# Reordering VectorE's work at the start of a fused layer: the third x tile's statistics placed behind the PSUM copy of the second tile's transposed x

## The chip, the cores and the metric

The kernel runs on one core of one Trainium2 chip. The metric is device time in microseconds (us) of one execution; lower is better. "Span" is the time from the first to the last instruction in the trace; the device time is about 1.8 us longer than the span. Each timed execution also reports its mean granted TensorE clock. 3.41 us at half clock in a span of 366 us lower the mean by 0.5 x 3.41 / 366 = 0.0047, so such an execution reads 0.995, as the profiled one of the kernel before does, instead of 1.00.

Engines: PE is TensorE's matmuls, PEld its weight loads, DVE is VectorE, ACT is ScalarE, POOL is GpSimd, SP is SyncE, which issues most DMAs.

## The reference, cut to what matters

```python
x = A_x                                     # 1 x 2048 x 576, bf16
h = x + attention(layernorm(x), wqkv, wo)   # 32 heads, each token sees 8 tokens, 2 apart
h2 = h + mlp(layernorm(layernorm(h)), w1, b1, w2, b2)   # 576 -> 4608 -> 576, gelu
return h2
```

The 2048 tokens are 16 tiles of 128. The change touches only the first 10 us: layernorm of the first x tiles, their transposition, and the first k and v products.

## The kernel before

Tiles are named by position in `EVEN`, the list of even tiles: "first tile" is `EVEN[0]`. An even tile is centered on VectorE, transposed on TensorE into PSUM, copied to SBUF (`xnT`), and multiplied with wqkv. The factor 1/sigma is applied when ScalarE evacuates the product from PSUM.

```python
# loads are issued in this order on SyncE's queue (t = 1 is k, t = 2 is v, t = 0 is q)
load_x(EVEN[0:1]); load_x(EVEN[1:2])
# ... the two tail pieces of wk go through ScalarE's queue
load_wqkv(1, 0, 2); load_wqkv(1, 2, KF)      # wk
load_x(EVEN[2:3]); load_x(EVEN[3:4])         # third and fourth x tile
load_wqkv(2, 0, 2); load_wqkv(2, 2, KF)      # wv
for r in range(2):
    load_wqkv_half(nc.sync, 2, r)
load_x(EVEN[4:6])                            # fifth and sixth x tile
# ... further loads; then 13 matmuls of constants that keep TensorE busy from 0.78 us

def ln1_even_stats(gi):      # bn_stats x2, bn_aggr on VectorE
    ...
def ln1_even_center(gi):     # x - mean, on VectorE
    ...
def ln1_even(gi):
    ln1_even_stats(gi)
    ln1_even_center(gi)

def ln1_even_rstd(*gis):
    for gi in gis:
        ...
        nc.vector.tensor_scalar(out=veps[:], ...)              # var + eps, VectorE
        rstd_of[EVEN[gi]] = ln_rstd(veps, f"ln1_{gi}", 1)[:, 0:1]   # pow(-0.5), GpSimd

def tr_x(js, tag):
    ...                      # transposes on TensorE into a PSUM pair
    copy = nc.vector.tensor_copy if j == EVEN[1] else nc.scalar.copy
    copy(out=xnT[j][:, k0:k1], in_=...)      # the second tile's copy is VectorE's
```

A "visit" makes the products of two (tile, k/v/q) pairs, each in two halves. The second half must come after the whole first half, and a no-operation on GpSimd carries that order: it waits for the first half's last matmul, and TensorE's second half waits for it.

```python
def marker(mm_ins):
    nop = nc.gpsimd.nop().ins
    tc.add_manual_dep(nop, mm_ins.name, sync_dep, ...)
    return nop

def visit(makes, ...):
    def first(make):
        duos.append(make())
        marks.append(marker(phase(duos[-1], 0, None)))
    ...                                      # first halves of all, then:
    phase(duos[n], 1, marks[n])              # second half, behind the marker
    duos[n]["evac"]()                        # ScalarE: PSUM -> SBUF, times 1/sigma
```

The instructions of each engine run in the order in which the program states them: in the trace of before, VectorE's copy, whose input was ready at 6.38 us, ran at 8.11 us, behind the statistics stated ahead of it. The start of the main part reads:

```python
ln1_even(0)                  # first tile: statistics and centering on VectorE
ln1_even_act(1)              # second tile: statistics on ScalarE, centering on VectorE
seq = [(j, t) for t in (1, 2) for j in EVEN[:2]] + [(j, 1) for j in EVEN[2:]] + ...

ln1_even_stats(2)            # third tile
tr_x(EVEN[0:1], "D")
tr_x(EVEN[1:2], "C")
ln1_even_center(2)
ln1_even_rstd(0, 1)
for qd in range(len(seq) // 2):
    duos = [qkv_duo(*seq[2 * qd]), qkv_duo(*seq[2 * qd + 1])]
    visit(duos, hooks.get(qd), ...)
    call(after.get(qd, ()))  # from here: other tiles' statistics, attention of finished tiles
```

Later parts: attention's first product of a tile on VectorE; SyncE's queue, which reloads the k of that tile and then stores, transposes and loads the odd tiles' x (`xd`, `xnT`); and the output projection `pw`, whose input `oT` is written by VectorE, stored to DRAM and loaded back transposed.

## Time and profile before

| | before |
|---|---|
| median of 3 timed runs | 366.63 us (366.52 to 367.52) |
| profiled execution | 367.94 us, span 366.2 us, mean clock 0.995 |
| TensorE busy | 360.4 us, 98% of the span |
| VectorE busy | 299.1 us, 82% |
| ScalarE busy | 229.1 us, 63% |

The profile's chain follows the work that ended last back from the end, with each engine's share of the span. The first line is for engines:

```profile
PE 88%; DVE 7%; DMA 3%; SPq 1%; issue 0%; POOL 0%
```

TensorE is the bound, and any idle TensorE time before the end is a candidate. The view of waits for TensorE lists only these (who waited, for whom: us in total, times, longest):

```profile
PE pq L215 <- DVE xnT L270: 1.3, 1, 1.3
PE busy L772 <- PEq L1061: 0.8, 1, 0.8
PE pw L215 <- DMA oT<-td: 0.2, 1, 0.2
```

The first is the target of the change. The timeline of VectorE around it (start, duration, engine, line, operation; in brackets the idle time before the instruction and what ended it):

```profile
4.57 0.36 DVE L789 TENSOR_SCALAR q_all<-x_all,ln_nmean 128x576 bf16<-128x576 bf16 x1
7.13 0.82 DVE L149 BATCH_NORM_STATS2 ln_stats<-x_all 128x6 f32<-128x288 bf16 x2 [2.20 <-DMA x_all<-in_A_x_dram]
7.98 0.21 DVE L150 BATCH_NORM_AGGREGATE ln_mv<-ln_stats 128x2 f32<-128x12 f32 x1
8.11 0.44 DVE L270 COPY xnT<-xt_pt 128x640 bf16<-128x640 bf16 x1
8.46 0.36 DVE L789 TENSOR_SCALAR q_all<-x_all,ln_mv 128x576 bf16<-128x576 bf16 x1
8.74 0.15 DVE L819 TENSOR_SCALAR ln_veps<-ln_mv 128x1 f32<-128x1 f32 x1
8.80 0.14 DVE L819 TENSOR_SCALAR ln_veps<-ln_sq 128x1 f32<-128x1 f32 x1
```

VectorE idles 2.20 us, because the third tile's statistics (L149) are next and its load has not landed. The copy (L270) stands behind them, although TensorE's timeline shows that its transposes (L182, L186) ended at 6.14 + 0.24 = 6.38 us:

```profile
6.14 0.24 PE L186 MATMUL xt_pt<-ident,q_all 128*64 128x128 bf16 x1
6.31 0.83 PE L215 MATMUL pq<-wq_sb,xnT 64*128 64x288 bf16 x8
6.97 0.30 PE L215 MATMUL pq<-wqh_sb,xnT 64*128 64x288 bf16 x2
8.60 0.95 PE L215 MATMUL pq<-wq_sb,xnT 64*128 64x288 bf16 x8 [1.33 <-DVE xnT L270]
9.34 0.45 PE L215 MATMUL pq<-wqh_sb,xnT 64*128 64x288 bf16 x2
9.58 2.95 PE L215 MATMUL pq<-wq_sb,xnT 64*128 64x288 bf16 x24
```

Note the last line too: 24 matmuls in 2.95 us. The windows view of three equal stretches says why; they are cut where the trace's own clock records begin (5.43, 8.85 and 12.26 us). Its columns are the stretch and its length, then busy time and instruction count of PE, PEld, DVE, ACT and POOL, then the granted clock, the DMA share and GB/s:

```profile
5.43:8.85 3.42, 2.09 (x24) 1.14 (x24) 1.69 (x7) 0.75 (x2) 0.00 (x0) 1.00 1.02 315
8.85:12.26 3.41, 3.41 (x34) 2.21 (x30) 2.48 (x10) 1.19 (x2) 1.08 (x2) 0.50 1.00 321
12.26:15.67 3.41, 3.41 (x50) 2.27 (x48) 3.27 (x14) 2.13 (x4) 1.06 (x2) 1.00 1.07 359
```

After a stretch with TensorE busy 2.09 of 3.42 us, the clock was halved for exactly one stretch of 3.41 us. Three more lines are VectorE's first product of attention, its first sum with the projection, and TensorE's wait for oT:

```profile
26.86 2.56 DVE L343 TENSOR_TENSOR prod<-kv_ring,q_all 128x4608 bf16<-128x4608 bf16 x1 [0.22 <-ACT q_all L310]
54.83 0.76 DVE L459 TENSOR_TENSOR h<-pw,x_all 128x576 f32<-128x576 f32 x1 [0.52 <-PE pw L215]
88.14 0.54 PE L215 MATMUL pw<-wo_sb,oT 64*128 64x288 bf16 x6 [0.21 <-DMA oT<-td]
```

### The profile page before, as it was taken

What the parts mean: (1) busy time and instruction counts of PE and PEld (TensorE: products, weight loads), DVE (VectorE), ACT (ScalarE), POOL (GpSimd) and SP (SyncE); (2) the same over time, 40 slices, a digit from 0 to 9 for tenths busy, and PEclk for the clock granted to TensorE, in tenths of its full rate; (3) what the DMA queues carried; (4) which work ended last, traced back from release to release, by engine and by line L of the source; (5) the groups of instructions that cost most, each with busy time, mean ns of one, the idle gap of its engine ahead of it and who ended that gap; (6) DMA issues with size and microseconds to landing.
All of it is one profiled execution on the core that took longest, in us unless ns stands there. A gap on an engine that the chain in (4) does not pass through costs nothing.

```text
span 366.2 us, 11427 instructions
## 1 busy us (share of the span) xinstructions
PE 360.4 (98%) x4899; PEld 291.3 (80%) x4899; DVE 299.1 (82%) x422; ACT 229.1 (63%) x507; POOL 38.3 (10%) x47
## 2 busy tenths in 40 slices
PE   7999999999999999999999999999999999999996
PEld 3677877788778877887788778878887888778874
DVE  4889999999899999999999898989995599710331
ACT  4579865799545674468546864686468646625630
POOL 1232003000120030102110021011101010100000
PEclk9899999999999999999999999999999999999999
DMA  7977989973444853630452145303631452030001
GB/s 241 306 197 260 236 216 215 370 270 71 137 107 80 165 198 70 108 98 34 129 109 71 38 103 117 90 32 92 130 72 35 81 93 56 3 90 18 2 2 33
DMA packets 61908, 43.70 MB, mean 119 GB/s; under 512 B 31889, under 2 KB 60177, under 8 KB 61857
## 3 DMA queue, kind: packets, MB, share of 16 engines
q1 hardware_dynamic: 59968, 41.13, 41.2%
q0 software_dynamic: 1728, 1.77, 4.7%
q8 instruction: 38, 0.62, 0.7%
q10 hardware_dynamic: 160, 0.07, 0.1%
q14 instruction: 14, 0.11, 0.1%
HBM read 21.10 MB, written 12.42 MB: 92 GB/s over the span
## 4 chain that ended last, share of the span: by engine, by line
PE 88%; DVE 7%; DMA 3%; SPq 1%; issue 0%; POOL 0%
PE pm L215 34%; PE po L659 27%; PE pq L215 11%; PE po L574 10%; PE pw L215 5%; DVE prod L349 1%; DVE prod L343 1%; DMA oT<-td 1%; DMA x_all<-in_A_x_dram 1%; DVE prod L395 1%; DVE ln_stats L149 1%; DVE prod L401 1%; PE xt_pt L182 1%; SPq L104 0%; DMA td<-q_all 0%; DVE h L459 0%
## 5 line engine op out<-in xcount | busy, mean ns | idle before, releaser
L555 ACT ACTIVATE h_all<-pm,b_sb 128x256 f16<-128x256 f32 (+1 forms) x288 | 108.3, 496 | 77.1 <-PE pm L215 77.1
L215 PE MATMUL pm<-hnT,w_sb 64*128 64x256 bf16 x2304 | 143.0, 269 | 0.0
L215 PEld LDWEIGHTS <-w_sb 64*128 64x128 bf16 x2304 | 111.7, 94 | 15.1 <-issue 1.7
L659 PEld LDWEIGHTS <-h_all 128*128 128x128 f16 x544 | 52.3, 98 | 15.3 <-issue 2.5
L215 PE MATMUL pq<-wq_sb,xnT 64*128 64x288 bf16 x768 | 56.0, 288 | 1.3 <-DVE xnT L270 1.3
L215 PEld LDWEIGHTS <-xnT 64*128 64x128 bf16 x864 | 42.3, 96 | 13.4 <-DVE xnT L270 1.6
L349 DVE TENSOR_TENSOR prod<-prod 128x2304 bf16<-128x2304 bf16 (+1 forms) x64 | 44.2, 691 | 2.1
L659 PE MATMUL po<-w2a_sb,h_all 128*128 128x288 bf16 (+1 forms) x312 | 43.6, 286 | 0.0
L395 DVE TENSOR_TENSOR prod<-kv_ring,probs 128x4608 bf16<-128x4608 bf16 x16 | 40.9, 2553 | 1.3 <-DMA kv_ring<-kv_dram 0.9
L343 DVE TENSOR_TENSOR prod<-kv_ring,q_all 128x4608 bf16<-128x4608 bf16 x16 | 40.8, 2549 | 0.4 <-ACT q_all L310 0.2
L215 PE MATMUL pm<-hnT,w1h_sb 64*128 64x256 bf16 x288 | 39.2, 269 | 0.0
L401 DVE TENSOR_TENSOR prod<-prod 128x2304 bf16<-128x2304 bf16 (+1 forms) x32 | 33.8, 1057 | 1.0
L574 PEld LDWEIGHTS <-h_all 128*128 128x128 bf16 x288 | 27.9, 98 | 7.9 <-issue 1.0
L479 POOL TENSOR_TENSOR ln_rstd<-ln_var,mhalf 128x1 f32<-128x1 f32 x13 | 14.2, 1091 | 178.0 <-ACT ln_var L478 178.0
L574 PE MATMUL po<-w2a_sb,h_all 128*128 128x288 bf16 x224 | 28.5, 286 | 0.0
L659 PEld LDWEIGHTS <-kv_ring 128*128 128x128 f16 x240 | 23.5, 98 | 5.9
L659 PE MATMUL po<-w2b_sb,h_all 128*128 128x288 bf16 (+1 forms) x152 | 22.2, 286 | 0.0
L639 DVE TENSOR_TENSOR kv_ring<-h_all 128x1536 f16<-128x1536 f16 (+3 forms) x10 | 6.9, 686 | 16.0 <-ACT h_all L555 16.0
L215 PE MATMUL pw<-wo_sb,oT 64*128 64x288 bf16 x256 | 19.5, 283 | 0.2 <-DMA oT<-td 0.2
L162 POOL TENSOR_TENSOR ln_rstd<-ln_veps,mhalf 128x1 f32<-128x1 f32 (+2 forms) x14 | 12.5, 903 | 51.2 <-DVE ln_veps L156 30.6
L215 PEld LDWEIGHTS <-oT 64*128 64x128 bf16 x288 | 13.4, 94 | 5.3 <-issue 1.7
L459 DVE TENSOR_TENSOR h<-pw,x_all 128x576 f32<-128x576 f32 x16 | 11.5, 752 | 6.5 <-PE pw L215 6.5
(107 smaller groups left out, 374.6 us busy)
## 6 DMA issues: line engine op xcount, KB each, us to landing
w_sb<-in_B_w_dram SPq DMA_DIRECT2D x6, 768.0 KB, 5.7
kv_ring<-kv_dram SPq DMA_DIRECT2D x28, 144.0 KB, 2.8
w2a_sb<-in_B_w_dram SPq DMA_DIRECT2D x4, 1008.0 KB, 6.7
kv_dram<-kv_ring SPq DMA_DIRECT2D x13, 288.0 KB, 3.6
out_dram<-o_sb SPq DMA_DIRECT2D x15, 144.0 KB, 2.2
td<-q_all SPq DMA_DIRECT2D x14, 144.0 KB, 2.2
td<-hn SPq DMA_DIRECT2D x14, 144.0 KB, 1.8
x_all<-in_A_x_dram SPq DMA_DIRECT2D x12, 144.0 KB, 2.8
```

The lines of the kernel that those rows point to most:

```text
L162: nc.gpsimd.tensor_tensor(out=rstd[:], in0=veps[:], in1=mhalf[:].to_broadcast([P, n]), op=ALU.pow)
L215: last = nc.tensor.matmul(duo["g"][r ^ swap][i], lhsT=lhsT, rhs=rhs, start=(swap == 0 and i == 0 and kt == 0), stop=(swap == 1 and kt == K ...
L343: nc.vector.tensor_tensor(out=prod[:], in0=k_ring[j % 2], in1=q_all[:, j, :].unsqueeze(1) .to_broadcast([P, W, D]), op=ALU.mult)
L349: nc.vector.tensor_tensor(out=prod[:, :, o * H:o * H + n], in0=prod[:, :, a * H:a * H + n], in1=prod[:, :, c * H:c * H + n], op=ALU.add)
L395: nc.vector.tensor_tensor(out=prod[:].rearrange("p w (d h) -> p w d h", h=H), in0=v_ring[j % 2].rearrange("p w (d h) -> p w d h", h=H), in ...
L401: nc.vector.tensor_tensor(out=prod[:, 0:n, :], in0=prod[:, 0:n, :], in1=prod[:, n:2 * n, :], op=ALU.add)
L459: nc.vector.tensor_tensor(out=h[:].rearrange("p (g c) -> p g c", g=2), in0=pw[:, :, 0:HALF], in1=x_of(j).rearrange("p (g c) -> p g c", g=2 ...
L479: nc.gpsimd.tensor_tensor(out=rstd[:], in0=var[:], in1=mhalf[:], op=ALU.pow)
L555: pace[0] = nc.scalar.activation(out=hT(grp)[:, f, 0:N], in_=ps[:, r, i * N:(i + 1) * N], func=ACT.Gelu_apprx_tanh, bias=b1_sb[:, f:f + 1] ...
L574: nc.tensor.matmul(banks[half], lhsT=hT(grp)[:, f, i * P:(i + 1) * P], rhs=w2_rows(f)[:, half * HALF:(half + 1) * HALF], start=(f == 0), s ...
L639: nc.vector.tensor_tensor(out=s_slot(t, m0, m1), in0=a, in1=b, op=alu)
L659: nc.tensor.matmul(bank, lhsT=l, rhs=r, start=start, stop=stop, skip_group_check=True)
```

## The change

The intent is to let the copy, and the small var + eps operations of the first two tiles, run while VectorE waits for the third tile's load anyway.

```diff
-        ln1_even_stats(2)
+        ln1_even_rstd(0, 1)
         tr_x(EVEN[0:1], "D")
         tr_x(EVEN[1:2], "C")
-        ln1_even_center(2)
-        ln1_even_rstd(0, 1)
+        ln1_even(2)
         for qd in range(len(seq) // 2):
```

No instruction is added or removed. On VectorE three instructions move ahead of the statistics; GpSimd's order does not change.

## The prediction

> **What bounds the kernel now.** The engine table gives TensorE (PE) 360.4 of 366.2 us busy (98%), VectorE (DVE) 299.1. The chain of waits is 88% PE, 7% DVE, 3% DMA. PE has two idle stretches of note: 1.33 us from 7.27, released by DVE's copy of the second tile's transposed x, and 0.21 at 88, released by a DMA. Its clock was halved once: the windows view shows 0.50 from 8.85 to 12.26 us, where 24 matmuls took 2.95 us that later take 1.64. [...]
>
> **Why the gap.** The timeline shows DVE idle from 4.93 to 7.13 us: the third tile's statistics wait for that tile's load (landed 7.10). The queue is in order; the copy stands behind them and runs at 8.11 (0.44 us), although its transposes ended near 6.4.
>
> **What the change does.** Same 391 DVE rows; only the order at the start changes: two small var+eps operations (0.15 us each) and the copy (0.44 us) go into DVE's idle hole before the load lands. The copy should run at 6.4 to 6.9. The statistics stay bound by their load, near 7.13.
>
> **What that is worth.**
> - PE: the gap goes (1.3 us), and probably the half-clock window (36 matmuls in 4.05 us, about 2.35 at later rates: 1.7 us). The next visit then meets the loads of the v weights, which landed at 8.43 to 9.75 (new waits 0.2 to 0.5 us). PE should be 2.5 to 2.8 us early by the transposes that now start at 12.58.
> - Most of it is lost again. From 11.11 us (load of the fifth tile) DVE is a nearly unbroken stream to 88; up to 64 only three of its pauses can shrink: 0.52 (26.47), 0.22 (26.86), 0.52 (54.83) = 1.26 us. PE's next meeting with it is the projection at 88.14, which waits for oT, stored and read back after DVE's sum at 81.4. So PE waits there 1 to 1.6 us more. From there PE has no slack: at most about 1.3 us of the span is left.
> - [...] An untouched clock alone would win that 1.26 us, leaving the change almost nothing. The times (366.52, 366.63, 367.52), beside 367.94 for the profiled, throttled execution, allow that the median was unthrottled. I mix: 1.3 us if throttled, 0.1 if not.
>
> **Predicted: 366.0 us, range 364.9 to 366.9 (8 in 10).** Faster by over 2%: 0.01; within 2%: 0.98; slower by over 2%: 0.01.
>
> **What will show it.** Right: the copy at 6.4 to 6.9 us, PE without a gap over 0.5 us before 12, granted clock 1.00 between 8 and 13, transposes of the third tile near 10 us, DVE's first product of attention near 26.1 instead of 26.86, the wait for oT near 88 grown to over 1 us, span about 365. Wrong: a half-clock stretch within the first 15 us; a DVE stream that starts no earlier; the projection at 88.14 moving by the full 2.7 us.
>
> **What would make it wrong.** The longer wait near 87 us may itself [...] halve the clock (1.7 us lost: no gain, or 0.5 us slower). Shifted ScalarE evacuations could move paced loads. Or all timed runs are throttled, and the gain is the full 1.3 us.

The gap (1.3 us) and the half-clock stretch (1.7 us), less the new waits (0.2 to 0.5 us), are the 2.5 to 2.8 us; the cap leaves about 1.3 us, for a throttled execution, and 0.1 us stands for one at full clock. Mixed, they take about 0.6 us off the 366.63 us of before: 366.0 us.

## The result, and the profile after

| | before | after |
|---|---|---|
| median of 4 runs of the same rounds | 366.57 us (365.90 to 367.52) | 365.19 us (365.08 to 365.28) |
| ratio | | 0.996, interval 0.9938 to 0.9983 |
| profiled execution | span 366.2 us, clock 0.995 | span 363.3 us, clock 1.00 |

A ratio is the mean time of one kernel's fast runs over that of the other's in the same rounds, so it is not quite the ratio of the medians. The interval excludes 1, so the change is faster, by about 0.4% (in microseconds the interval is 0.6 to 2.3).

The two profiles differ by 2.9 us of span, twice as much as the medians. That is the first warning: the profile of before fell in an execution with a half-clock stretch, and most executions have none (e1 below).

The chain after is TensorE nearly alone:

```profile
PE 98%; DMA 1%; DVE 0%; ACT 0%; SPq 0%; issue 0%
```

TensorE's waits shrink to the one at the program's start:

```profile
PE busy L772 <- PEq L1060: 0.8, 1, 0.8
```

VectorE's timeline after: the small operations and the copy run in the hole, and the copy now waits for the transposes themselves:

```profile
4.76 0.15 DVE L819 TENSOR_SCALAR ln_veps<-ln_mv 128x1 f32<-128x1 f32 x1
5.35 0.15 DVE L819 TENSOR_SCALAR ln_veps<-ln_sq 128x1 f32<-128x1 f32 x1 [0.45 <-ACT q_all L811]
6.83 0.49 DVE L270 COPY xnT<-xt_pt 128x640 bf16<-128x640 bf16 x1 [1.33 <-PE xt_pt L186]
7.24 0.81 DVE L149 BATCH_NORM_STATS2 ln_stats<-x_all 128x6 f32<-128x288 bf16 x2
```

TensorE's timeline after has no gap, and 24 matmuls take 1.71 us; the transposes of the third tile start at 9.98 us, against 12.58 before:

```profile
6.73 0.67 PE L215 MATMUL pq<-wq_sb,xnT 64*128 64x288 bf16 x8
7.23 0.29 PE L215 MATMUL pq<-wqh_sb,xnT 64*128 64x288 bf16 x2
7.38 0.66 PE L215 MATMUL pq<-wq_sb,xnT 64*128 64x288 bf16 x8
8.01 1.71 PE L215 MATMUL pq<-wq_sb,xnT 64*128 64x288 bf16 x24
9.98 0.28 PE L182 MATMUL xt_pt<-ident,q_all 128*128 128x128 bf16 x2
```

The windows view of the same two stretches of time: busy throughout, no half clock from 6.59 us on.

```profile
5.43:8.85 3.42, 3.42 (x44) 2.29 (x44) 2.02 (x7) 0.84 (x3) 0.67 (x2) 1.00 1.02 321
8.85:12.26 3.41, 3.41 (x46) 2.14 (x42) 2.86 (x11) 2.32 (x4) 0.16 (x1) 1.00 1.07 347
```

The 1.00 of its first line must be read with care. This trace's first clock record begins at 6.59 us, and the column says 1.00 before it by default. The first transposes show that TensorE was still slow there (after, then before, whose record begins at 5.43 us):

```profile
5.90 0.71 PE L182 MATMUL xt_pt<-ident,q_all 128*128 128x128 bf16 x5
5.75 0.45 PE L182 MATMUL xt_pt<-ident,q_all 128*128 128x128 bf16 x5
```

That is why the copy ran at 6.83 us here, and at 6.08 us in e2, where the two tiles' groups of five transposes took 0.44 and 0.45 us instead of the 0.69 and 0.71 here.

And the three later places:

```profile
25.09 2.55 DVE L343 TENSOR_TENSOR prod<-kv_ring,q_all 128x4608 bf16<-128x4608 bf16 x1
52.47 0.75 DVE L459 TENSOR_TENSOR h<-pw,x_all 128x576 f32<-128x576 f32 x1
85.27 0.66 PE L215 MATMUL pw<-wo_sb,oT 64*128 64x288 bf16 x8
```

So TensorE is 12.58 - 9.98 = 2.60 us early at the third tile, and still 88.14 - 85.27 = 2.87 us early at the projection. VectorE is 1.77 us early at attention and 2.36 us early at 52 us. In this pair of traces the lead was not lost on VectorE, as the prediction had said it would be.

### The profile page after: what moved, and what is told of

Its sections match the earlier page's. It is cut to its first block, busy times and chain, and to the rows that moved or that the text cites. A ratio compares the mean times of both kernels' runs of the same rounds, so it can differ in the third digit from the quotient of the medians.

```text
span 363.3 us, 11427 instructions
## 1 busy us (share of the span) xinstructions
PE 359.0 (99%) x4899; PEld 292.3 (80%) x4899; DVE 299.1 (82%) x422; ACT 229.3 (63%) x507; POOL 39.4 (11%) x47
## 3 DMA queue, kind: packets, MB, share of 16 engines
q0 software_dynamic: 1728, 1.77, 4.6%
## 4 chain that ended last, share of the span: by engine, by line
PE 98%; DMA 1%; DVE 0%; ACT 0%; SPq 0%; issue 0%
PE pm L215 39%; PE po L659 27%; PE pq L215 15%; PE po L574 10%; PE pw L215 5%; PE xt_pt L182 1%; DMA x_all<-in_A_x_dram 1%; PE xt_pt L186 0%; ACT q_all L810 0%; PE h_pt L182 0%; PE o_pt L182 0%; DVE o_sb L690 0%; SPq L104 0%; DVE q_all L789 0%; PE h_pt L186 0%; PE o_pt L186 0%
## 5 line engine op out<-in xcount | busy, mean ns | idle before, releaser
L215 PE MATMUL pq<-wq_sb,xnT 64*128 64x288 bf16 x768 | 54.4, 283 | 0.0
L162 POOL TENSOR_TENSOR ln_rstd<-ln_veps,mhalf 128x1 f32<-128x1 f32 (+2 forms) x14 | 13.4, 962 | 47.9 <-DVE ln_veps L156 31.6
L503 POOL DMA_DIRECT2D x_all<-h x12 | 10.9, 1060 | 54.6 <-DMA x_all<-in_A_x_dram 25.0
```

Source lines behind the costliest of these rows:

```text
L162: nc.gpsimd.tensor_tensor(out=rstd[:], in0=veps[:], in1=mhalf[:].to_broadcast([P, n]), op=ALU.pow)
L215: last = nc.tensor.matmul(duo["g"][r ^ swap][i], lhsT=lhsT, rhs=rhs, start=(swap == 0 and i == 0 and kt == 0), stop=(swap == 1 and kt == K ...
L503: ins = nc.gpsimd.dma_start(out=x_of(j), in_=h_of.pop(j)[:], accum_op=ALU.add).ins
```

## The experiments

All experiments have five rounds. The kernel before was timed in every set, on the same chip, and the ratios below are against it. Because sets fell on different chips, I compare kernels of different sets by their distance from the kernel before of their own set. I take before's executions at a clock above 0.996 for this. Their medians in the four sets are 365.89, 366.06, 365.80 and 365.93 us.

### e1: the kernel before, as a subject of its own

No edit; one profile and five timed runs with their clocks.

> The kernel before, unchanged, run as a subject of its own, so that every timed run shows its granted clock. Theory A (the gap of 1.33 us in TensorE's matmuls also costs a half-clock window in some executions): runs fall in two groups, clock 0.995 or 0.996 with a span near 366, and clock 1.00 with a span near 364.3 to 365. Rival B (the clock is a bystander): the spans do not follow the clock; spread of about 1.5 us within equal clocks. The ratio to the kernel before is 1.000 within 0.002 either way.

Measured: 366.14, 366.06, 365.95 and 365.46 us at clock 1.00, and 367.31 us at 0.995; ratio 0.9996. The profiled execution took 2120.91 us; it is left out. Its trace has a span of 2119.1 us, the 13 matmuls that open the kernel take 12.13 us instead of the 4.11 in before, and TensorE is busy for 20.00 of 20 us in three samples, from 500, 1000 and 2000 us; the clock column reads 1.00, and why it was slow is not shown. In the four sets together the kernel before ran 42 times. Seven executions read 0.995, with a median of 367.73 us (367.27 to 368.08). The other 35 have a median of 365.93 us, and all but one lie between 365.46 and 366.48. The two groups do not overlap but for that one, 367.30 us at 0.999, which the clock does not explain. Theory A's two groups are there; the clock costs 367.73 - 365.93 = 1.8 us, in one execution of six.

### e2: only the statistics move

```diff
-        ln1_even_stats(2)
         tr_x(EVEN[0:1], "D")
         tr_x(EVEN[1:2], "C")
-        ln1_even_center(2)
+        ln1_even(2)
         ln1_even_rstd(0, 1)
```

> Only the statistics move behind the copy; the two var+eps operations stay where they were, behind the third tile's centering. Theory A (the early copy is all of the gain): as fast as the changed kernel, near 365.2 us, 1.2 to 1.6 us under the kernel before, no gap of TensorE over 0.5 us before 12 us. Rival C (the gain comes from the early 1/sigma of the first two tiles, which frees PSUM evacuations on ScalarE): no gain or less than 0.5 us.

Measured: 365.54 us (365.30 to 365.76), ratio 0.9978 (0.9956 to 1.0), no execution at 0.995; 0.35 us under before's clock-1.00 median. By the ratio the gain is 0.8 us, between the two theories' numbers; by the medians it is about 0.4 us, within rival C's. The trace has something that neither had named. The waits of TensorE in this kernel:

```profile
PE pq L215 <- POOLq L225: 1.0, 1, 1.0
PE pq L215 <- DMA wq_sb<-in_A_wqkv_dram: 0.4, 1, 0.4
```

TensorE now waits for GpSimd's queue at L225, the marker. The 1/sigma operations of the first two tiles stand ahead of the markers in that queue; their inputs come at 8.69 + 0.14 us, behind the third tile's centering, and TensorE's second halves start at 8.95 us. The copy alone moves the wait from VectorE's queue to GpSimd's.

### e3: only the var + eps operations move

```diff
+        ln1_even_rstd(0, 1)
         ln1_even_stats(2)
         tr_x(EVEN[0:1], "D")
         tr_x(EVEN[1:2], "C")
         ln1_even_center(2)
-        ln1_even_rstd(0, 1)
```

> Only the two var+eps operations move to the front; the statistics stay ahead of the copy. Theory A: the time of the kernel before within 0.4 us, and the gap of 1.3 us in TensorE stays. Rival C: most of the 1.4 us gain.

Measured: 366.30 us (365.75 to 367.65), ratio 1.0008 (0.9983 to 1.0032); two of six executions at 0.995. TensorE's gap is still 1.3 us in the view of waits. No gain: this half of the change does nothing alone, and rival C falls.

### e4: the kernel before, with the gap filled

```diff
+        def fill():
+            more = psum_pair("D", "busy_more")
+            for _ in range(5):
+                nc.tensor.matmul(more[:, 0, :], lhsT=ones[:, 0:P], rhs=ones[:], start=True, stop=True)
+
+        hooks[0] = {1: fill}
         for qd in range(len(seq) // 2):
```

> The kernel before with five unused matmuls of 512 columns in the gap [...], so that the gap stays in time but TensorE does not idle in it. Results stay right. Theory A: the clock stays at 1.00 from about 6 us on in every run, and the time is that of the best runs of the kernel before, 0.5 to 1.2 us under its median, with a spread of 0.3 us; the changed kernel stays a little better. Rival B (only the 1.33 us of gap counts, not the clock): no change from the kernel before.

Measured: 365.84 us (365.45 to 365.91), ratio 0.9985 (0.9966 to 1.0005); all six clocks at 0.999 or 1.00. No execution is in the slow group (with one in six expected, none of six is no proof), and the median equals before's clock-1.00 executions (365.89 in this set). In its trace the five unused matmuls took 1.26 us. The expected 0.5 to 1.2 us under before's median did not come, because that median is itself an execution at full clock.

### e7 and e12: the gap doubled, then the doubled gap filled

e7 puts two unused statistics operations ahead of the copy in the kernel before; e12 adds nine unused matmuls in the gap, as in e4.

```diff
         ln1_even_stats(2)
+        junk(2)          # two bn_stats on the first tile's x, result unused
         tr_x(EVEN[0:1], "D")
```

> The kernel before with two more unused statistics operations (0.82 us) ahead of the copy, so that TensorE's gap grows from 1.33 to about 2.15 us. Theory A: executions with a half-clock window become the majority, and their share, not only 0.8 us of delay, moves the time: median 1.5 to 2.5 us over the kernel before, fast-clock executions 0.5 to 0.8 us over its own. Rival B: 0.5 to 0.8 us slower in all executions, with no more of them at 0.995.

> The kernel with the doubled gap (2.07 us in its trace, 5 of 6 executions at clock 0.994 or 0.995, median 368.27 us) with nine unused matmuls of 512 columns in the gap [...]. The gap in useful work stays as long; only TensorE's idleness goes. Theory A [...]: no execution at 0.995, and 366.5 to 367.2 us, 1.1 to 1.8 us under the kernel with the doubled gap. Rival B (only the length of the gap counts): 368 us or more.

Measured: e7 took 368.27 us (367.08 to 368.63), ratio 1.0048 (1.0026 to 1.007). Five of its six executions read 0.994 or 0.995 (368.01 to 368.63 us); the sixth, at 1.00, took 367.08. e12 took 366.54 us (366.51 to 366.83), all five at 0.998 or above; in its trace the nine unused matmuls took 2.14 us. The windows view of e7, two stretches of 3.41 us:

```profile
6.98:10.39 3.41, 1.34 (x21) 0.85 (x21) 3.03 (x11) 0.00 (x0) 0.50 (x1) 1.00 0.95 283
10.39:13.80 3.41, 3.41 (x31) 1.99 (x25) 3.20 (x13) 1.48 (x2) 0.58 (x2) 0.50 1.00 325
```

and of e12, the same two:

```profile
6.98:10.39 3.41, 3.41 (x33) 1.79 (x31) 3.34 (x12) 0.00 (x0) 0.84 (x2) 1.00 1.01 313
10.39:13.80 3.41, 3.41 (x50) 2.26 (x47) 3.23 (x13) 2.44 (x4) 1.01 (x3) 1.00 1.07 358
```

The useful work is held up about as long in both: the second tile's matmuls start at 9.52 us in e7 and at 9.18 us in e12. Above before's full-clock executions of their own sets the two stand at 2.21 and 0.61 us, so 1.6 us go with TensorE's idleness (at most 0.3 of it with the later start). This is the clearest evidence that the clock is a cause, and that TensorE's idleness in the gap triggers it. The share of half-clock executions rises with the gap: none of the ten of the changed kernel, 7 of 42 at 1.33 us, 5 of 6 at 2.07 us.

### e5: the changed kernel again

> The changed kernel once more, to stand beside the others of this set. Expected 365.1 to 365.3 us, no execution with the clock at 0.995, spread under 0.4 us.

Measured: 365.36 us (365.06 to 366.27), ratio 0.9976 (0.9955 to 0.9997), none at 0.995, 0.70 us under before's 366.06. One execution at 366.27 (clock 0.999) makes the spread wider than expected.

### e6 and e9: VectorE made longer in the changed kernel

Two or six unused statistics operations (0.82 or 2.45 us) ahead of attention's first product:

```diff
-            5: [..., c_(ln1_bias, 9), c_(att_qk_a, A[0])],
+            5: [..., c_(ln1_bias, 9), c_(junk, 2), c_(att_qk_a, A[0])],     # 6 in e9
```

> The changed kernel with two unused statistics operations (0.82 us together) on VectorE just ahead of attention's first product. In its trace oT landed at 85.16 us and TensorE took it at 85.27, so VectorE's stream has about 0.1 us of slack there. Theory D (VectorE's stream is at its limit in the changed kernel): slower by 0.5 to 0.8 us, near 365.9, with a wait of TensorE for oT near 86 us. Rival P (only TensorE bounds it): slower by less than 0.2 us.

> The changed kernel with six unused statistics operations (2.45 us) on VectorE ahead of attention's first product. With two of them (0.82 us) the median rose by only 0.26 us, because the transposing load of oT, issued later, took 3.1 us instead of 4.0. Theory S (VectorE's stream has about 1 us of slack in the changed kernel, then it binds): 1.0 to 1.9 us slower than the changed kernel, near 366.4 to 367.2 us, with a wait of TensorE for oT of 0.8 to 1.6 us near 86 us. Theory D (no slack): 2.3 us or more. Rival P (VectorE does not bind at all): under 0.4 us.

Measured: e6 365.62 us (365.14 to 367.61), ratio 0.9988, 0.26 us over the changed kernel in the same set, which is not clear of the spread of either; e9 366.73 us (366.29 to 369.33), ratio 1.0033. e9's four executions at clock 1.00 have a median of 366.38 us, 0.58 over before's 365.80, while the changed kernel was 0.70 under its own: a cost of about 1.3 us for 2.45 us of work. So theory S holds in size: VectorE has some slack, up to roughly a microsecond, and then it binds. The place is not the one I expected. e9's wait of TensorE for oT does not appear; what appears in its timeline is a wait for the odd tiles' transposed x, twice, 1.0 us in all; the longer wait is the 0.69 us before this line:

```profile
37.97 0.66 PE L215 MATMUL pq<-wq_sb,xnT 64*128 64x288 bf16 x8 [0.69 <-DMA xnT<-xd]
```

Two of e9's six executions read 0.995 and took 369.04 and 369.33 us; neither was profiled, so where their clock fell is not known.

### e8: the markers ahead of 1/sigma

As e2, with the same order on VectorE, but 1/sigma behind the markers in GpSimd's queue.

```diff
         ln1_even(2)
-        ln1_even_rstd(0, 1)
+        hooks[0] = {2: c_(ln1_even_rstd, 0, 1)}   # after the first visit's two markers
```

> As the kernel that moved only the statistics, with the same order on VectorE, but the first two tiles' 1/sigma stand behind the two marker operations in GpSimd's queue instead of ahead of them. In that kernel TensorE waited 0.98 us for GpSimd's queue. Theory E (the early var+eps operations of the change matter only because the markers stand behind 1/sigma in GpSimd's queue): the wait is gone, the transposes of the third tile come near 10 us, and the time is that of the changed kernel within 0.2 us. Rival C (the later 1/sigma costs by itself, through ScalarE's PSUM evacuations): it stays at 365.5 us, with a new wait of TensorE for ScalarE near 10.5 us.

Measured: the wait for GpSimd's queue is gone from TensorE's waits, which in this kernel are:

```profile
PE busy L772 <- PEq L1060: 0.8, 1, 0.8
PE pq L215 <- DMA wq_sb<-in_A_wqkv_dram: 0.5, 1, 0.5
```

That settles what e2's wait was. The time does not settle its worth: 365.65 us, but from 364.92 to 366.25, ratio 0.9982 (0.9958 to 1.0005), 0.41 us under before where the changed kernel of the same set was 0.70 under. In e8 ScalarE's first evacuation waits for 1/sigma until 9.44 us, against 8.77 in the changed kernel, but TensorE did not wait for ScalarE. Theory E is shown for the wait and open for the time. The third tile's transposes came at 10.52 us and not near 10, and the traces say why: in after, e5, e6, e8, e9 and e11 they start 0.25 to 0.26 us after the last piece of the v weights has landed (9.73 and 9.98 us in after, 10.10 and 10.35 in e5, 10.26 and 10.52 in e8). Once the copy and the markers are early, this landing ends last, and in e8's profiled execution it was late.

### e10: the v weights' landing taken out (wrong result)

```diff
-                c0 = t * D + g * HALF
-                return xt[sl, kt, :], (wq_sb[sl, kt, c0:c0 + HALF] if kt < KF else wqh_sb[sl, t, :])
+                w = 1 if (j, t) == (EVEN[0], 2) else t
+                c0 = w * D + g * HALF
+                return xt[sl, kt, :], (wq_sb[sl, kt, c0:c0 + HALF] if kt < KF else wqh_sb[sl, w, :])
```

> Wrong result on purpose: in the changed kernel the first tile's v is multiplied with the k weights, which are there, so that TensorE's third visit no longer meets the v weights' loads (waits of 0.2 to 0.5 us in the traces so far). Theory V (the landing of the v weights took the rest of the closed gap): 0.2 to 0.5 us faster than the changed kernel, near 364.9 us, transposes of the third tile near 9.6 us. Rival D (VectorE or oT holds the end of the stage): no gain, and a longer wait for oT near 86 us.

Measured (result wrong): 364.65 us, ratio 0.9961 (0.9937 to 0.9985), 1.15 us under before's 365.80, against 0.70 for the changed kernel in its set: about 0.45 us came from no longer meeting the v weights (a difference of two sets). In its trace the third tile's transposes start at 9.16 us, before the last piece of these weights lands (9.81). But 365.63 and 367.19 us stand beside five runs between 364.40 and 364.74. The 367.19 one was profiled, at clock 1.00, and its timeline shows what it met:

```profile
39.09 0.66 PE L215 MATMUL pq<-wq_sb,xnT 64*128 64x288 bf16 x8 [2.75 <-DMA xnT<-xd]
```

TensorE was there at 36.34 us, only 0.75 us earlier than in the changed kernel's trace, where the load of xnT landed at 37.05 us and TensorE took it at 37.09. In this execution the load landed at 39.05 us, 2.0 us later. VectorE was not the reason: it began attention at 25.11 us, against 25.09. SyncE's queue was 1.3 us behind at the reload of k before it (29.33 against 28.05), and the load itself took 5.5 us instead of 4.3; why is not known. So the odd tiles' x is a second limit right behind the first, with 0.04 us to spare in the changed kernel's trace. It may also explain the rare long executions of other kernels at full clock, but those were not profiled.

This trace also corrects the picture of the clock. TensorE idles 2.75 us, longer than the 2.07 us in e7, and no half-clock stretch follows. Two stretches of 3.41 us that meet inside the gap:

```profile
34.50:37.91 3.41, 1.85 (x32) 1.25 (x26) 3.24 (x6) 2.89 (x5) 0.00 (x0) 1.00 1.11 275
37.91:41.32 3.41, 2.23 (x38) 1.95 (x40) 3.18 (x8) 0.46 (x2) 0.00 (x0) 1.00 0.77 230
```

TensorE was busy 1.85 of 3.41 us in the first, less than the 2.09 of 3.42 us after which before's clock was halved. So busy time alone does not decide.

### e11: the v weights loaded ahead of the fourth tile

```diff
         load_x(EVEN[2:3])
-        load_x(EVEN[3:4])
         load_wqkv(2, 0, 2)
         load_wqkv(2, 2, KF)
         for r in range(2):
             load_wqkv_half(nc.sync, 2, r)
+        load_x(EVEN[3:4])
```

> A try at a better kernel: the load of the fourth x tile is issued behind the v weights' loads, which should land about 0.4 us earlier. Theory V gives TensorE up to 0.3 us of it; but the fourth tile's statistics then start near 9.9 us and its transposes may wait, and VectorE's stream starts up to 0.8 us later, within its slack if theory S is right. Between 0.3 us faster and 0.3 us slower than the changed kernel; over 0.5 us slower would speak for theory D.

Measured: 365.21 us (364.66 to 365.74), ratio 0.9971 (0.9949 to 0.9993), 0.59 us under before's 365.80, where the changed kernel is 0.70 under in its set. The v weights' last piece landed at 9.59 us (9.73 in the changed kernel's trace), TensorE still waited 0.4 us for them, and the fourth tile's transposes waited 0.2 us for VectorE. No difference from the changed kernel can be told from noise. No version tried with a right result beats the changed kernel.

## Why the prediction was right or wrong

**Right: the mechanism at the start.** The copy ran at 6.83 us (predicted 6.4 to 6.9), the gap went, the clock stayed at 1.00, the third tile's transposes came at 9.98 us (predicted near 10), and the new waits for the v weights were there (0.2 to 0.5 us in e5, e6, e8, e9 and e11; in after itself too short to be listed; worth about 0.45 us by e10). e2 and e3 together add what the prediction missed: the var + eps operations are not a bystander. Without them TensorE waits 0.98 us at the markers in GpSimd's queue; with them alone nothing is gained. Only together do they clear the way for TensorE.

**Right: the clock is a lottery, and the timed median was not throttled.** The prediction called it possible that the median of before had run at full clock. e1 and the other sets show it for most: 35 of 42 executions did. (The clocks of the first set, with its 366.63 us, are not on record; that time lies under every throttled one, 367.27 us or more.) The stretches at half clock last 3.41 us and start at 8.85 us in the trace of before and at 10.39 us in that of e7. e7 and e12 show that TensorE's idleness in this gap is the trigger: with a gap of 2.07 us left idle, 5 of 6 executions read 0.994 or 0.995; with the gap filled, none of 5. By what rule the clock falls is not shown.

**Wrong: "Most of it is lost again ... at most about 1.3 us of the span is left".** This step failed. The prediction summed three pauses of VectorE (0.52 + 0.22 + 0.52 = 1.26 us) and let VectorE's stream and oT cap the gain. Measured between the two traces, VectorE was 2.36 us early at 52 us. 0.62 us of the difference is that the stream started earlier: the fifth tile's statistics started at 10.49 instead of 11.11 us, when their load landed. This is scatter and not the change, since kernels with the old order have it too (the load landed at 10.54 us in e4, at 10.49 in e7). The remaining 2.36 - 0.62 - 1.26 = 0.48 us are a pause near 24.6 us that I had not counted (0.20 us) and a few hundredths around each of the three. In addition the transposing load of oT took 4.6 us from issue to landing in before, 4.0 in after and 3.1 in e6: its length absorbs part of a late VectorE (issued at 82.1 us in e6 and 81.1 in after, it landed at about 85.2 in both). So the wait near 88 us that was to grow over 1 us disappeared; in the changed kernel's trace oT landed at 85.16 us, 0.11 us before TensorE took it. e4 shows that VectorE's lateness was not a limit of the old order: with that order at full clock, oT landed at 85.44 us instead of 88.09, and TensorE took it at 85.97. e6 and e9 measure the slack directly: 0.82 us more on VectorE cost 0.26 us (within the spread), 2.45 us cost about 1.3.

**Wrong: "0.1 if not" throttled.** From before's executions at full clock the change gains 0.70 us in e5's set, not 0.1. The gap is 1.33 us; the v weights give back about 0.45 of it.

**Why the number still held.** The prediction was 366.0 us with 364.9 to 366.9; measured were 365.19 and, in e5, 365.36. It mixed 1.3 us for throttled and 0.1 us for full-clock executions. The measured terms are larger: about 0.7 us against an execution at full clock, and 0.7 + 1.8 = 2.5 us against one with a half-clock stretch, which is one of six; on average 0.7 + 1.8 / 6 = 1.0 us. The first set measured more, 1.38 us between the medians, within the interval of its ratio (0.6 to 2.3 us); the clocks of its executions of before are not on record, so what the rest is stays open. Both terms were too small by the same failed step, the cap through VectorE. That the number held is luck: the range was wide enough, and the sum behind it was not right.

**Left open.** Why most executions of before escape the half clock is not shown: no escaped one with the gap was profiled. What makes rare executions at full clock 1 to 2 us long (367.30 of before, 366.27 of e5, 367.61 of e6) is known only for e10's, which was profiled: a late load. Whether e8's order costs anything is not resolved.

## What to carry to other kernels

When an engine's next instruction waits for a load, look at what stands behind it in the same queue that could already run, and follow every queue in which the released engine's own order is carried: here a marker on GpSimd would have kept most of the wait had its inputs not moved too. A short TensorE gap can cost more than its length, and only in some executions (the gap of 1.33 us cost the clock, 1.8 us, in one of six, a 2.75 us one in e10's trace did not); read the granted clock of every timed run before you set a profile against a median. Before you cap a gain by the next engine's stream, measure its slack with a few unused instructions, since summed pauses of one trace mixed a load's scatter with real limits.
